# The last route of a mixture-of-experts takes along lanes and table of the route in front; a limit compared from PSUM; the order of four steps changed

## The chip, the cores and the metric

One core of a Trainium2 chip. The metric is the device time of one execution in microseconds (us), the median of several. The engines run side by side and keep each its own program order: TensorE (PE in the rows, PEld its weight loads), VectorE (DVE), ScalarE (ACT), GpSimd (POOL); SyncE (SP) issues most DMAs, POOL the gathers.

## What is computed

A linear attention with decay gives x, a mixture of 8 experts with one expert per token follows, and a gated MLP ends it. Batch 2, sequence 768, width 384 (8 heads of 48), expert width 1024, all in float32. The part that matters here is how the expert of a token is found:

```python
logits = x @ w_gate
local_gate = sigmoid(x @ w_local)
for s in range(S):                       # for each of the 2 sequences
    fresh_e = argmax(logits[b, s])
    e = fresh_e if s == 0 or local_gate[b, s] < 0.5 else prev_e
    prev_e = e
    p = softmax(logits[b, s])
    out[b, s] = p[e] * (relu(x[b, s] @ w1[e]) @ w2[e])
```

## The kernel before

**Attention.** The sequence is cut into 6 chunks of 128 tokens (`c`), each for 2 batches (`b`). For a chunk the kernel makes scaled keys and queries (`prep`: `kt`, `rh`, on DVE or POOL), scores on PE (`scores`, tile `pa`), a mask on DVE (`mask`, tile `am`), and in `mix` the product with the values (`py`), the part from the running state `st`, and the update of the state (`pst`, added on DVE). The token's own term comes from `diag` (`ku` on POOL, its sum `ad` on DVE) and `own` (`av`, on ACT, or on POOL for the last). `rows` adds it to `py` and writes 128 rows of x to DRAM (`xd`). A buffer `py` can be written again only when its `rows` has read it.

**Routes.** `route` gives each token its expert and its place in that expert's list. It is a generator, and each `yield` ends a step that the calling code places between other work. It runs for the groups of chunks (0, 1), (2, 3), (4,), (5,). Its steps: the logits plus own gates and the bit "takes a fresh expert" (`rb`, `ro`, DVE); counts of those bits (`pz`, PE); the best expert (`mx` to `oh`, DVE); a selection matrix `sel` (DVE), which picks for each token the row of its last fresh token, and `cz`, the expert carried in from the chunk in front, for tokens that `nz` marks; the experts `oes` (PE, then DVE) and `od`, the same times the token's number; places in the lists (PE, DVE: `rks`); `lane`, for each token a row of 256 with a one at its place (a comparison on DVE with `board.lanes`, the numbers 0 to 255); and the product of `lane` and `od` on PE, which is added to `table`. For the last group that sum goes to `rowid`, the row numbers by which the gathers fetch the experts' tokens (`x_fetch`, indirect DMA on POOL, tile `xe`). Small results of all routes lie in one PSUM bank, the tile `board`. The framework orders PE's writes to that bank behind every DVE access that stands in front of them in the program, and the other way round.

**The end of the attention.** Before the last routes are done, part of expert 0 is begun: `first_part` (in the code `lead`) turns the first half of the gathered rows (`tx`), multiplies them with the first weights (`h`, 24 products of 128 columns, in 8 steps) and those with the second weights (`o`, 24 products), with the turning of the second half after 15 of them. `FILL` says how many steps of `lead` stand between two steps of the last route. The weights of the experts come by DMA and are split into a high and a low part (ACT casts, DVE or POOL subtracts, line 321). After that come expert by expert `layer1` and `layer2`, then the gather of the results and the gated MLP; both are PE's work from end to end.

**A count check.** After the first route `limit` compares two of the counts with 128 (line 268): more would send the kernel to a general version.

Of the kernel before, what the change touches and what calls it, by code (L numbers as in the profile page):

```python
# [9 lines left out]
F32 = mybir.dt.float32  # L10
F32R = mybir.dt.float32r
BF16 = mybir.dt.bfloat16
F16 = mybir.dt.float16
# [3 lines left out]
ALU = mybir.AluOpType  # L17
# [4 lines left out]
B = 2  # L22
# [5 lines left out]
E = 8  # L28
FF = 1024
C = 128  # L30
NC = S // C
CAP = 256
HC = CAP // 2
NE = 2
NF = 4
# [2 lines left out]
WS = 3072  # L38
LC = D + G
WARM = 22  # L40
FILL = (0, 3, 1, 0, 1, 1, 0)
WMIN = 0.6
WMAX = 1.1

# [2 lines left out]
def rwkv_moe_gmlp(ctx, tc, a, out):  # L47
# [94 lines left out]
                return x.rearrange("t (g e) -> t g e", e=shape[1])  # L142
            return x

    def route(cs, board, lg, more, sm, ps):

        n = len(cs)
        c = cs[-1]
        N = n * B
        turn = turn_of(c)  # L150

        def small(nm, shp, dt=F32):
            return sm.tile([128, 2 * B] + shp[2:], dt, name=nm, tag=nm)[:, 0:N]
# [4 lines left out]
        def bc(t):  # L158
            return t.unsqueeze(2).to_broadcast([128, N, E])
# [32 lines left out]

        mx = small("mx", [128, N])
        ve.tensor_reduce(mx, l8, axis=AX.X, op=ALU.max)
        ve.tensor_tensor(sc, l8, bc(mx), op=ALU.is_equal)
        ex = board.exs[:, B * cs[0]:B * cs[0] + N]
        ve.tensor_tensor(ex, l8, bc(mx), op=ALU.subtract)
        ve.tensor_tensor(sc, sc, rev.unsqueeze(1).to_broadcast([128, N, E]), op=ALU.mult)
        m2 = small("m2", [128, N])
        ve.tensor_reduce(m2, sc, axis=AX.X, op=ALU.max)  # L200
        oh = small("oh", [128, N, E], BF16)
        ve.tensor_tensor(oh, sc, bc(m2), op=ALU.is_equal)
        se.activation(ex, ex, AF.Exp)
        yield
        cc = small("cc", [128, N])
        ve.tensor_copy(cc, pc)
        sel = [sm.tile([128, B, 2, C], BF16, name=f"sel{j}", tag=f"sel{j}", bufs=1) for j in range(n)]
        for j in range(n):
            for b in range(B):
                g = B * j + b  # L210
                ve.tensor_scalar(sel[j][:, b, j:n], pr[:, b, j:n], cc[:, g:g + 1], ro[:, g:g + 1],
                                 op0=ALU.is_equal, op1=ALU.mult)
        if cs[0]:

            ve.tensor_scalar(nz, pc, 0.0, None, op0=ALU.is_equal)
            cz = small("cz", [128, N, E])
            for j in range(n):
                g = slice(B * j, B * j + B)
                ve.tensor_tensor(cz[:, g], carry, nz[:, g].unsqueeze(2).to_broadcast([128, B, E]), op=ALU.mult)
        yield  # L220
        for b in range(B):
            for j in range(n):
# [2 lines left out]
                              start=(i == 0), stop=(i == j))  # L225
        pe.matmul(pf, lhsT=same, rhs=count.unsqueeze(1).to_broadcast([128, N, E]), start=True, stop=False)
        yield
        oe = board.oes[:, B * cs[0]:B * cs[0] + N]
        if cs[0]:
            ve.tensor_tensor(oe, cz, pq, op=ALU.add)  # L230
# [13 lines left out]
            pe.matmul(pn_, lhsT=ones, rhs=oe[:, g], start=(g == 0), stop=(g == N - 1))  # L244
        pe.matmul(pl, lhsT=last, rhs=oe[:, N - B:N], start=True, stop=True)
        yield
        rk = board.rks[:, B * cs[0]:B * cs[0] + N]
        rt_ = small("rt", [128, N, E])
        ve.tensor_tensor(rt_, oe, pf, op=ALU.mult)
        ve.tensor_reduce(rk, rt_, axis=AX.X, op=ALU.add)  # L250
        lane = sm.tile([128, 2 * B, CAP], F16, name="lane", tag="lane", bufs=1)
        for g in range(N):
            ve.tensor_scalar(lane[:, g], board.lanes, rk[:, g:g + 1], None, op0=ALU.is_equal)
        yield
        for h in range(2):
            for g in range(N):
                pe.matmul(pt_[:, h], lhsT=lane[:, g, 128 * h:128 * h + 128], rhs=od[:, g],
                          start=(g == 0), stop=(g == N - 1))

        ve.tensor_tensor(rowid if c == NC - 1 else table, table, pt_, op=ALU.add)  # L260
        ve.tensor_tensor(count, count, pn_, op=ALU.add)
        ve.tensor_copy(carry, pl)
        if c == NF - 1:

            ve.tensor_scalar(count[:, 0:1], count[:, 0:1], HC, None, op0=ALU.max)
            ve.tensor_copy(rowid[:, 0, 0:1], table[:, 0, 0:1])
        if c == NE - 1:
            ve.tensor_scalar(limit[:, E + 1:], count[:, E - 2:E], HC, None, op0=ALU.is_gt)
        yield

    def places(board, sm):
# [101 lines left out]
    def x_fetch(e, part=range(2), rows_read=B * S):  # L373
        if e not in xe:
            xe[e] = xep.tile([128, 2, DM], F32, name="xe", tag="xe")
        for m in part:
            po.indirect_dma_start(  # L377
                out=xe[e][:, m], out_offset=None, in_=xd[0:rows_read],
                in_offset=bass.IndirectOffsetOnAxis(ap=rowid[:, m, e:e + 1], axis=0))


    with ExitStack() as att:
# [94 lines left out]
        def prep(c, b):  # L477

            t = loads[c]
            rh[c, b] = wk.tile([128, NP, C], F32, name="rh", tag=f"rh{b}")  # L480
            kt[c, b] = wk.tile([128, NP, C], F32, name="kt", tag=f"kt{b}")
            if c + b == 0:
                def ready(n):
                    o = slice(n // 2, n) if n == C else slice(0, n)
                    if n >= C // 2:
                        ve.tensor_tensor(kt[0, 0][:, :, o], t["kT"][:, 0, :, o], ktab[:, :, o], op=ALU.mult)

                powers(ready)
                po.tensor_tensor(rh[0, 0], t["rT"][:, 0], rtab, op=ALU.mult)
                return  # L490
            (ve if c * b < 2 else po).tensor_tensor(kt[c, b], t["kT"][:, b], ktab, op=ALU.mult)
            po.tensor_tensor(rh[c, b], t["rT"][:, b], rtab, op=ALU.mult)

        def prep_keys(c, b=slice(0, B)):
# [113 lines left out]
        def first_part():  # L608

            def turned(m):  # L610
                t = ps1.tile([128, 3, 128], F32, name="tx", tag="pg")
                for k in range(3):
                    pe.transpose(t[:, k], xe[0][:, m, 128 * k:128 * k + 128], ident)
                return t

            t = turned(0)
            x = wk.tile([128, 3, 128], F32, name="xl", tag="x0")
            se.copy(x, t)
            yield
            part = [ld.tile([128, 8, 128], F32R, name="hp", tag=n) for n in ("kT", "rT")]  # L620
            hs = [ps1.tile([128, 4, 128], F32, name="h", tag=f"pa{g}") for g in range(2)]
            for f in range(8):
                for k in range(3):
                    pe.matmul(hs[f // 4][:, f % 4], lhsT=whole[:, k, 128 * f:128 * f + 128], rhs=x[:, k],
                              start=(k == 0), stop=(k == 2))
                yield
                if f == 4:
                    hf = wk.tile([128, 4, 128], F32, name="hf", tag="am")
                    se.activation(hf, hs[0], AF.Relu)
                    se.copy(part[0][:, 0:4], hf)  # L630
                    po.tensor_tensor(part[1][:, 0:4], hf, part[0][:, 0:4], op=ALU.subtract)
            se.activation(part[0][:, 4:8], hs[1], AF.Relu)
            ve.scalar_tensor_tensor(part[1][:, 4:8], hs[1], 0.0, part[0][:, 4:8], op0=ALU.max, op1=ALU.subtract)
            w2 = slot[1].rearrange("p j (k f) -> p j k f", k=8)
            o = ps1.tile([128, DM], F32, name="o", tag="pst")
            terms = sorted(((f, s, q) for f in range(8) for s, q in PASS), key=lambda x: x[1])
            for n, (f, s, q) in enumerate(terms):
                if n == 15:
                    se.copy(xf, turned(1))
                pe.matmul(o, lhsT=part[s][:, f], rhs=w2[:, q, f], start=(n == 0), stop=(n == 23))  # L640
                if n % 6 == 5:
                    yield
            ob = wk.tile([128, DM], F32, name="of", tag="x1")
            se.copy(ob, o)
            sy.dma_start(out=ys[0:HC, :], in_=ob)
# [28 lines left out]
        with tc.manual_schedule():  # L674
# [44 lines left out]
            for c in range(1, NC - 1):  # L719
# [20 lines left out]
                next(rt, 0)  # L740
                own(c, 0)
                y0 = mix(B * c)
                next(rt, 0)
                next(rt, 0)
                rows(c - 1, 1, y1)
                own_gates(c, 0)
                scores(B * c + 2)
                gates(c + 1, 1)
# [36 lines left out]
            old = [rt]  # L785
            next(rt)
            lead = first_part()
            scores(B * c + 1)
            next(dg)
            own(c, 1)  # L790

            def tabled():
                next(old[0])
                x_fetch(0, [0], NF * B * C)
                logits(c - 1, 1, y1)
                g = (c - 1,)
                old.append(route(g, board, xr[g, "l"], als[g], sm, ps1))
                next(old[1])

            y0 = mix(B * c, {0: tabled, 3: lambda: next(old[1])})  # L800
# [13 lines left out]
                logits(c, 0, y0)  # L814

            y1 = mix(B * c + 1, {2: experts, 3: lambda: next(rt)})
            next(rt)
            own_gates(c, 0)
            logits(c, 1, y1)
            old.append(route((c,), board, xr[(c,), "l"], als[(c,)], sm, ps1))  # L820
            rt = old[2]
            next(rt)
            rows(c, 0, y0)
            rows(c, 1, y1)
            w_split(0, 3, po, 1)
            w_fetch(1, 2)
            next(lead)
            next(old[1])
            next(rt)
            for n in FILL:  # L830
                next(rt)
                for _ in range(n):
                    next(lead, 0)
            x_fetch(0, [1])
            for _ in range(4):
                next(lead, 0)
            x_fetch(1)
            places(board, sm)
# [631 lines left out]
```

## Time and profile before

| | |
|---|---|
| runs (us) | 368.22, 368.73, 371.37; median 368.73 |
| the profiled execution: own time / span | 371.84 / 370.0 us |
| PE busy | 354.5 us (96% of the span) |
| DVE / ACT / POOL busy | 63% / 48% / 46% |
| mean granted TensorE clock | 0.98 |

The profile is of one execution, and its span reaches from its first instruction to its last. A busy share is a mean over stages with different limits; here the stages from 100 us on show no idle PE but for the hand-over between experts and MLP, and the attention shows idle PE in a few places, so the rows below are of those places.

### The profile page before, as it was taken

The numbers are of one execution on the slowest core, as the hardware profiler recorded it, in microseconds if no ns is written. First come the engines' busy times: TensorE is split into PE (matmuls) and PEld (weight loads), VectorE is DVE, ScalarE is ACT, GpSimd is POOL, SyncE is SP. The second block draws the span as 40 slices with busy tenths as digits, with TensorE's granted clock in tenths as the row PEclk, the third lists the DMA queues.
The fourth block names the chain that finished last, engine by engine and source line by source line (L and its number), as shares of the span: only waits on it lengthen the run. The fifth ranks groups of instructions, "written<-read, shape, count | busy, mean of one in ns | idle before, by whom it ended". The sixth has DMA issues, their size and how long they took to land.

```text
span 370.0 us, 6477 instructions
## 1 busy us (share of the span) xinstructions
PE 354.5 (96%) x2485; PEld 339.6 (92%) x2485; DVE 233.7 (63%) x429; ACT 175.9 (48%) x344; POOL 170.0 (46%) x105
## 2 busy tenths in 40 slices
PE   7999999798999999999999999999999999999992
PEld 3899999787899999999999999778999999999992
DVE  7486997997468879898989843356777223234000
ACT  4439666535278582928374353344568310102321
POOL 4779995925478966556464032441000431311000
PEclk9589999999999999999999999999999999999997
DMA  6978999032599999989897311535302000000321
GB/s 200 388 297 291 379 396 365 4 128 87 153 317 350 304 300 355 336 262 309 282 325 257 142 64 33 178 110 170 130 4 83 0 2 0 3 0 2 109 93 64
DMA packets 34920, 67.27 MB, mean 182 GB/s; under 512 B 2688, under 2 KB 18816, under 8 KB 34880
## 3 DMA queue, kind: packets, MB, share of 16 engines
q1 hardware_dynamic: 33088, 61.27, 47.7%
q0 software_dynamic: 1792, 5.51, 4.9%
q8 instruction: 21, 0.34, 0.4%
q14 instruction: 19, 0.16, 0.1%
HBM read 56.54 MB, written 10.22 MB: 180 GB/s over the span
## 4 chain that ended last, share of the span: by engine, by line
PE 84%; DVE 6%; DMA 4%; issue 2%; ACT 1%; POOL 1%; POOLq 0%; ACTq 0%
PE h L983 16%; PE o L1033 15%; PE vs L1150 13%; PE po L1166 7%; PE v L1096 7%; PE u L1135 5%; PE py L604 5%; PE pa L561 4%; PE tx L901 2%; PE pst L588 2%; PE pg L503 2%; PE py L599 2%; DMA xe<-xd,rowid 2%; PE h L1012 1%; DMA xg<-ys,slots 1%
## 5 line engine op out<-in xcount | busy, mean ns | idle before, releaser
L321 POOL TENSOR_TENSOR slot<-raw,slot 128x1536 fp32r<-128x1536 f32 x17 | 61.4, 3613 | 88.7 <-ACT slot L319 88.5
L983 PE MATMUL h<-xt,slot 128*128 128x256 f32 x504 | 61.7, 283 | 0.0
L983 PEld LDWEIGHTS h<-xt,slot 128*128 128x128 f32 x504 | 61.3, 192 | 0.1
L1033 PE MATMUL o<-slot,ht 128*128 128x384 f32 x336 | 60.2, 336 | 0.0
L1033 PEld LDWEIGHTS o<-slot,ht 128*128 128x128 f32 x336 | 58.0, 188 | 0.0
L321 DVE TENSOR_TENSOR slot<-raw,slot 128x1536 fp32r<-128x1536 f32 x19 | 42.8, 2253 | 18.3 <-ACT slot L319 18.3
L319 ACT CAST slot<-raw 128x1536 fp32r<-128x1536 f32 x36 | 53.1, 1477 | 0.0
L1150 PE MATMUL vs<-slot,slot 128*128 128x384 f32 x288 | 50.1, 334 | 0.0
L1150 PEld LDWEIGHTS vs<-slot,slot 128*128 128x128 f32 x288 | 49.9, 188 | 0.0
L1096 PE MATMUL v<-slot,xT 128*128 128x512 f32 x108 | 27.6, 401 | 0.0
L1157 ACT CAST slot<-gv 128x768 fp32r<-128x768 f32 x8 | 6.7, 838 | 43.9 <-POOL gv L1156 39.5
L604 PE MATMUL py<-vx,am 128*128 128x128 f32 x192 | 26.0, 285 | 0.0
L1156 POOL TENSOR_TENSOR gv<-gv,uT 128x768 f32<-128x768 f32 x7 | 12.9, 1838 | 28.0 <-DVE gv L1154 28.0
L1135 PE MATMUL u<-xT,slot 128*128 128x384 f32 x144 | 25.4, 335 | 0.2 <-ACT uT L1140 0.2
L1135 PEld LDWEIGHTS u<-xT,slot 128*128 128x128 f32 x144 | 25.0, 188 | 0.6 <-ACT uT L1140 0.5
L377 POOL DMA_INDIRECT xe<-xd,rowid x16 | 23.5, 1469 | 3.8 <-issue 1.2
L1166 PE MATMUL po<-slot,slot 128*128 128x384 f32 x144 | 25.1, 334 | 0.0
L1166 PEld LDWEIGHTS po<-slot,slot 128*128 128x128 f32 x144 | 25.0, 188 | 0.0
L604 PEld LDWEIGHTS py<-vx,am 128*128 128x128 f32 x192 | 23.8, 199 | 0.0
L993 DVE SCALAR_TENSOR_TENSOR ht<-h,ht 128x512 fp32r<-128x512 f32 (+1 forms) x28 | 18.0, 647 | 8.5 <-ACT ht L992 8.3
L1096 PEld LDWEIGHTS v<-slot,xT 128*128 128x128 f32 x108 | 19.5, 188 | 3.7
L891 POOL DMA_INDIRECT xg<-ys,slots x12 | 12.0, 1003 | 23.2 <-DVE slot L321 11.2
(203 smaller groups left out, 560.1 us busy)
## 6 DMA issues: line engine op xcount, KB each, us to landing
raw<-w SPq DMA_DIRECT2D x30, 768.0 KB, 6.4
raw<-w_in SPq DMA_DIRECT2D x6, 768.0 KB, 6.6
ys<-ob SPq DMA_DIRECT2D x15, 192.0 KB, 5.0
kT<-kT SPq DMA_DIRECT2D x5, 512.0 KB, 6.1
rT<-rT SPq DMA_DIRECT2D x5, 512.0 KB, 8.1
vT<-vT SPq DMA_DIRECT2D x6, 384.0 KB, 6.4
v<-v SPq DMA_DIRECT2D x6, 384.0 KB, 8.2
k<-k SPq DMA_DIRECT2D x6, 384.0 KB, 8.1
```

The lines of the kernel that those rows point to most:

```text
L319: se.copy(hi, r)
L321: (eng or ve).tensor_tensor(lo, r, hi, op=ALU.subtract)
L377: po.indirect_dma_start(out=xe[e][:, m], out_offset=None, in_=xd[0:rows_read], in_offset=bass.IndirectOffsetOnAxis(ap=rowid[:, m, e:e + 1] ...
L561: pe.matmul(pa[h][:, p, :], lhsT=kt[c, b][64 * h:64 * h + 64, p, :], rhs=rh[c, b][64 * h:64 * h + 64, p, :], start=True, stop=True)
L604: pe.matmul(y[:, p], lhsT=m[:, h * NP + p, :], rhs=v[:, b, p, h, :], start=(c + p + h == 0), stop=(p == NP - 1 and h == 1))
L983: pe.matmul(h[:, j], lhsT=w1[:, s, k, 128 * f:128 * f + 128], rhs=xt[e][:, m, k], start=(n == 0), stop=(n == 8))
L993: ve.scalar_tensor_tensor(lo, x, 0.0, hi, op0=ALU.max, op1=ALU.subtract)
L1033: pe.matmul(o, lhsT=hidden(e, m, s, f), rhs=w2[:, q, f], start=(n == 0), stop=(n == 23))
L1096: pe.matmul(o, lhsT=xT[b][:, s, k, 128 * c:128 * c + 128], rhs=win[:, q, k, DF:FF], start=(n == 0), stop=(n == 8))
L1135: pe.matmul(o[:, h, 0:HS], lhsT=win[:, s, k, 128 * d:128 * d + 128], rhs=xT[b][:, q, k, HS * h:HS * h + HS], start=(n == 0), stop=(n == 8))
L1150: pe.matmul(o[:, h, 0:HS], lhsT=vn[b][:, s, k, 128 * d:128 * d + 128], rhs=wsp[q][:, k, HS * h:HS * h + HS], start=(n == 0), stop=(n == 17))
L1166: pe.matmul(o, lhsT=gt[b][:, s, k, 128 * c:128 * c + 128], rhs=wout[q][:, k], start=(n == 0), stop=(n == 11))
```

## The change

Six edits, all around the routes.

1. `limit` is compared from the sum in PSUM (`pn_`) instead of from `count` in SBUF.
2. In `route` the copy `cc` and the mark `nz` come right after `mx`, and `cz` in front of `m2`; before, they came at and after the selections.
3. In the loop over chunks `rows(c - 1, 1, y1)` comes in front of the two route steps behind `mix`.
4. `kt` of the last chunk's first batch is made on POOL instead of DVE.
5. At the last chunk the gather of the first half of expert 0's rows is issued in front of the own values (`own(c, 1)`); its one column of row numbers is written straight from PSUM, in front of `table`.
6. The route of chunk 4 stops when it has its places (`give`), and the last route (`take`) makes that route's lanes between its own steps, from a copy of the lane numbers in another PSUM bank (`held["lanes"]`), and does the products of both in one sum. `FILL` is new, and the first part's yields are finer: one product instead of three. The subtraction for `part[1]` goes behind the loop, and the last chunk's own gates go ahead of one route step.

```diff
-FILL = (0, 3, 1, 0, 1, 1, 0)
+FILL = (3, 0, 0, 7, 0, 1, 0, 5)
...
         ve.tensor_reduce(mx, l8, axis=AX.X, op=ALU.max)
+        if take:
+            take.pop("sums")()
+        cc = small("cc", [128, N])
+        ve.tensor_copy(cc, pc)
+        if cs[0]:
+            ve.tensor_scalar(nz, pc, 0.0, None, op0=ALU.is_equal)
         ve.tensor_tensor(sc, l8, bc(mx), op=ALU.is_equal)
...
+        if cs[0]:
+            cz = small("cz", [128, N, E])
+            for j in range(n):
+                g = slice(B * j, B * j + B)
+                ve.tensor_tensor(cz[:, g], carry, nz[:, g].unsqueeze(2).to_broadcast([128, B, E]), op=ALU.mult)
         m2 = small("m2", [128, N])
...
-        cc = small("cc", [128, N])
-        ve.tensor_copy(cc, pc)
         sel = [sm.tile([128, B, 2, C], BF16, name=f"sel{j}", tag=f"sel{j}", bufs=1) for j in range(n)]
...
+        def comparison(t, rk, g):
+            ve.tensor_scalar(t[:, g], take["lanes"] if take else board.lanes, rk[:, g:g + 1], None, op0=ALU.is_equal)
+
+        if take:
+            comparison(take["lane"], take["rk"], 0)
         oe = board.oes[:, B * cs[0]:B * cs[0] + N]
...
+        def sums():
+            ve.tensor_tensor(count, count, pn_, op=ALU.add)
+            ve.tensor_copy(carry, pl)
+        if take:
+            comparison(take["lane"], take["rk"], 1)
...
+        if give is not None:
+            give.update(lane=lane, rk=rk, od=od, sums=sums)
+            yield
+            return
...
+        pairs = [(lane[:, g], od[:, g]) for g in range(N)]
+        if take:
+            pairs = [(take["lane"][:, g], take["od"][:, g]) for g in range(B)] + pairs
...
+        if c == NF - 1:
+            ve.tensor_tensor(rowid[:, 0, 0:1], table[:, 0, 0:1], pt_[:, 0, 0:1], op=ALU.add)
         ve.tensor_tensor(rowid if c == NC - 1 else table, table, pt_, op=ALU.add)
...
-            ve.tensor_copy(rowid[:, 0, 0:1], table[:, 0, 0:1])
-        if c == NE - 1:
-            ve.tensor_scalar(limit[:, E + 1:], count[:, E - 2:E], HC, None, op0=ALU.is_gt)
+        if cs == tuple(range(NE)):
+            ve.tensor_scalar(limit[:, E + 1:], pn_[:, E - 2:E], HC, None, op0=ALU.is_gt)
...
-            (ve if c * b < 2 else po).tensor_tensor(kt[c, b], t["kT"][:, b], ktab, op=ALU.mult)
+            (ve if c * b < 2 and c < NC - 1 else po).tensor_tensor(kt[c, b], t["kT"][:, b], ktab, op=ALU.mult)
...
-                yield
+                    if f < 7 or k < 2:
+                        yield
...
                 y0 = mix(B * c)
+                rows(c - 1, 1, y1)
                 next(rt, 0)
                 next(rt, 0)
-                rows(c - 1, 1, y1)
...
+            held = {"lanes": ps1.tile([128, CAP // 2], F32, name="lanes", tag="pst").bitcast(F16)}
+            ve.tensor_copy(held["lanes"].bitcast(F32), lanes.bitcast(F32))
             scores(B * c + 1)
             next(dg)
-            own(c, 1)
             def tabled():
                 next(old[0])
                 x_fetch(0, [0], NF * B * C)
+                own(c, 1)
                 logits(c - 1, 1, y1)
...
             y1 = mix(B * c + 1, {2: experts, 3: lambda: next(rt)})
+            own_gates(c, 0)
             next(rt)
-            own_gates(c, 0)
...
-            next(lead)
-            next(old[1])
-            next(rt)
             for n in FILL:
-                next(rt)
                 for _ in range(n):
                     next(lead, 0)
+                next(rt)
             x_fetch(0, [1])
-            for _ in range(4):
+            for _ in range(9):
                 next(lead, 0)
             x_fetch(1)
```

On **DVE**, behind the first `mix` of chunk 4, where the route of chunks 2 and 3 runs, stood before:

```order
L194 TENSOR_REDUCE mx<-board 128x4
L195 TENSOR_TENSOR board<-board,mx 128x32
L197 TENSOR_TENSOR exs<-board,mx 128x32
L198 TENSOR_TENSOR board<-board,rev 128x32
L200 TENSOR_REDUCE m_984<-board 128x4
L202 TENSOR_TENSOR oh<-board,m_984 128x32
L206 COPY cc<-board 128x4
L211 TENSOR_SCALAR sel_991<-pz,cc,ro 128x256 x2
L211 TENSOR_SCALAR sel_992<-pz,cc,ro 128x128 x2
L215 TENSOR_SCALAR board<-board 128x4
L219 TENSOR_TENSOR cz<-carry,board 128x16 x2
L670 TENSOR_TENSOR x<-py,av 128x384
```

There stands now (line 696 is `rows`, line 222 the selections):

```order
L696 TENSOR_TENSOR x<-py,av 128x384
L195 TENSOR_REDUCE mx<-board 128x4
L199 COPY cc<-board 128x4
L202 TENSOR_SCALAR board<-board 128x4
L203 TENSOR_TENSOR board<-board,mx 128x32
L205 TENSOR_TENSOR exs<-board,mx 128x32
L206 TENSOR_TENSOR board<-board,rev 128x32
L211 TENSOR_TENSOR cz<-carry,board 128x16 x2
L213 TENSOR_REDUCE m_993<-board 128x4
L215 TENSOR_TENSOR oh<-board,m_993 128x32
L222 TENSOR_SCALAR sel_998<-pz,cc,ro 128x256 x2
L222 TENSOR_SCALAR sel_999<-pz,cc,ro 128x128 x2
```

The read of `py` moved from the end of this piece to its head, and `cc`, the mark (written to `board`) and `cz` moved in front of the selections.

On **PE**, at the end of the attention, the products of the two last routes stand between those of the first part (`h`, `o`). The rows are the first MATMUL of each kind in order, without the weight loads; before:

```order
L624 MATMUL h<-xl,whole 128x128 x3
L257 MATMUL board<-od,lane 128x8
L185 MATMUL pz<-up_65,rb 128x128
L624 MATMUL h<-xl,whole 128x128 x9
L224 MATMUL board<-oh,sel_1266 128x8
L624 MATMUL h<-xl,whole 128x128 x3
L239 MATMUL board<-oes,upst 128x16
L624 MATMUL h<-xl,whole 128x128 x6
L624 MATMUL h<-xl,whole 128x128 x3
L640 MATMUL o<-slot_105,hp 128x384 x15
L613 MATMUL tx<-ident,xe 128x128 x3
```

and now (`pz` belongs to the last route, `lane` to the last two):

```order
L649 MATMUL h<-xl,whole 128x128 x3
L186 MATMUL pz<-up_65,rb 128x128
L649 MATMUL h<-xl,whole 128x128 x7
L228 MATMUL board<-oh,sel_1264 128x8
L649 MATMUL h<-xl,whole 128x128
L248 MATMUL board<-oes,upst 128x16
L649 MATMUL h<-xl,whole 128x128 x5
L281 MATMUL board<-od,lane 128x8
L649 MATMUL h<-xl,whole 128x128 x8
L666 MATMUL o<-slot_105,hp 128x384 x15
L638 MATMUL tx<-ident,xe 128x128 x3
```

Before, the last route's four `lane` products stood between the rows x6 and x3 of `h`. The four of the route in front moved from ahead of `pz` to there, so that eight stand together; 7, 1, 5 and 8 products of the first part stand where 9, 3, 6 and 3 stood.

On **POOL**, from the split of the weights in chunk 3 on, stood before:

```order
L321 TENSOR_TENSOR slot_105<-raw,slot_105 128x1536
L492 TENSOR_TENSOR rh<-rT,rtab 128x512
L491 TENSOR_TENSOR kt<-kT,ktab 128x512
L520 TENSOR_TENSOR ku<-k,ub 128x768
L522 TENSOR_TENSOR ku<-ku,r 128x768
L535 TENSOR_TENSOR av<-vx_164,ad 128x456
L377 DMA xe<-xd,rowid 128x384
L668 TENSOR_TENSOR x<-x,av 128x384 x3
L631 TENSOR_TENSOR hp<-hf,hp 128x512
L377 DMA xe<-xd,rowid 128x384 x3
```

and now:

```order
L346 TENSOR_TENSOR slot_105<-raw,slot_105 128x1536
L516 TENSOR_TENSOR kt<-kT,ktab 128x512
L517 TENSOR_TENSOR rh<-rT,rtab 128x512
L545 TENSOR_TENSOR ku<-k,ub 128x768
L547 TENSOR_TENSOR ku<-ku,r 128x768
L402 DMA xe<-xd,rowid 128x384
L560 TENSOR_TENSOR av<-vx_164,ad 128x456
L694 TENSOR_TENSOR x<-x,av 128x384 x3
L657 TENSOR_TENSOR hp<-hf,hp 128x512
L402 DMA xe<-xd,rowid 128x384 x2
```

A multiplication `kt` is new in front of `rh` (each list leaves out the second `rh`, a second `kt` and a second split, which did not move), the gather of the first half went ahead of `av`, and that of the second half, which before was the first of the three at the end, went ahead of `hp`.

## Rows read from the trace of the kernel before

**Rows 1.** Windows, 100 to 225 us: length; PE, PEld, DVE, ACT, POOL; clock; DMA.

```profile
100.00:225.00 125.00, 125.00 (x910) 124.90 (x909) 100.01 (x100) 75.27 (x101) 70.54 (x26) 1.00 0.79 267
```

**Rows 2.** Windows, around the comparison, and the end of the attention whole.

```profile
62.50:66.70 4.20, 2.15 (x25) 1.81 (x24) 4.13 (x7) 2.62 (x10) 4.20 (x2) 1.00 0.42 159
62.50:98.20 35.70, 30.05 (x301) 28.00 (x299) 30.59 (x118) 14.60 (x47) 23.40 (x16) 1.00 0.32 107
```

**Rows 3.** Timeline, PE: start us, us, instruction, count, idle time before and its releaser.

```profile
66.61 0.50 PE L185 MATMUL pz<-up,rb 128*128 128x256 bf16 x4 [2.05 <-DVE rb L172]
74.74 1.16 PE L599 MATMUL py<-st,rh 128*128 128x128 f32 x8 [1.07 <-DVE x L670]
85.02 0.55 PE L613 MATMUL tx<-ident,xe 128*128 128x128 f32 x3 [0.50 <-DMA xe<-xd,rowid]
86.33 0.17 PE L239 MATMUL board<-oes,upst 128*128 128x16 bf16 x1 [0.16 <-DVE board L657]
88.49 0.24 PE L257 MATMUL board<-od,lane 128*128 128x8 f16 x4 [0.68 <-DVE ro L173]
91.41 0.19 PE L224 MATMUL board<-oh,sel 128*128 128x8 bf16 x2 [0.42 <-DVE cz L219]
98.17 0.52 PE L613 MATMUL tx<-ident,xe 128*128 128x128 f32 x3 [0.77 <-DMA xe<-xd,rowid]
```

**Rows 4.** Timeline, the comparison and its neighbours on PE, POOL and DVE.

```profile
62.37 3.43 POOL L321 TENSOR_TENSOR slot<-raw,slot 128x1536 fp32r<-128x1536 f32 x1 [4.41 <-ACT slot L319]
62.42 3.41 DVE L268 TENSOR_SCALAR limit<-count 128x2 f32<-128x2 f16 x1
63.67 0.89 PE L503 MATMUL pg<-wgb,vT 128*128 128x72 f32 x6
66.39 0.16 DVE L172 TENSOR_SCALAR rb<-board 128x4 bf16<-128x4 f32 x1
```

**Rows 5.** Timeline, POOL and DVE behind it, and the scores that use their tiles.

```profile
65.76 1.26 POOL L492 TENSOR_TENSOR rh<-rT,rtab 128x512 f32<-128x512 f32 x1
68.59 1.44 DVE L491 TENSOR_TENSOR kt<-kT,ktab 128x512 f32<-128x512 f32 x1
70.75 1.16 PE L561 MATMUL pa<-rh,kt 64*128 64x128 f32 x16
```

**Rows 6.** Timeline, DVE: the selections and the rows.

```profile
72.22 1.63 DVE L211 TENSOR_SCALAR sel<-pz,cc,ro 128x256 bf16<-128x256 f32 x4
74.14 0.55 DVE L670 TENSOR_TENSOR x<-py,av 128x384 f32<-128x384 f32 x1
```

**Rows 7.** Timeline, the table of chunks 2 and 3 and the first gather.

```profile
80.53 0.95 POOL L535 TENSOR_TENSOR av<-vx,ad 128x456 f32<-128x456 f32 x1 [6.92 <-DVE ad L525]
80.66 0.17 DVE L260 TENSOR_TENSOR table<-table,board 128x16 f32<-128x16 f32 x1 [0.27 <-PE board L257]
81.65 1.13 POOL L377 DMA_INDIRECT xe<-xd,rowid  x1 [0.17 <-DVE board L166]
```

**Rows 8.** Timeline, the last two routes and the first part.

```profile
87.04 0.61 DVE L253 TENSOR_SCALAR lane<-board,rks 128x256 f16<-128x256 f16 x2
88.21 0.16 DVE L172 TENSOR_SCALAR rb<-board 128x2 bf16<-128x2 f32 x1
88.73 2.25 PE L624 MATMUL h<-xl,whole 128*128 128x128 f32 x18
94.51 0.97 POOL L377 DMA_INDIRECT xe<-xd,rowid  x1 [0.34 <-DVE carry L262]
94.56 2.84 PE L640 MATMUL o<-slot,hp 128*128 128x384 f32 x15
```

**Rows 9.** SP's writes of x: the last three, landing of all twelve, of these three.

```profile
83.79 6.10 SPq L672 DMA_DIRECT2D xd<-x  x3
...
DMA to landing us min/median/max: 1.8/4.0/8.0
...
xd<-x SPq DMA_DIRECT2D x3, 192.0 KB, 1.9
```

More of the change, by code (lines that the diff above doesn't have):

```diff
@@ L143, in part, with route @@
             return x
-    def route(cs, board, lg, more, sm, ps):
+    def route(cs, board, lg, more, sm, ps, give=None, take=None):
         n = len(cs)
@@ L212, in route @@
                                  op0=ALU.is_equal, op1=ALU.mult)
[L213 to L219, printed above, removed]
         yield
@@ L250, in route @@
         ve.tensor_reduce(rk, rt_, axis=AX.X, op=ALU.add)
-        lane = sm.tile([128, 2 * B, CAP], F16, name="lane", tag="lane", bufs=1)
+        lane = take["lane"] if take else sm.tile([128, 2 * B, CAP], F16, name="lane", tag="lane", bufs=1)
+        if give is not None:
[3 more added lines that the diff above has]
+        if take:
+            lane = lane[:, B:2 * B]
         for g in range(N):
-            ve.tensor_scalar(lane[:, g], board.lanes, rk[:, g:g + 1], None, op0=ALU.is_equal)
+            comparison(lane, rk, g)
         yield
+        pairs = [(lane[:, g], od[:, g]) for g in range(N)]
+        if take:
+            pairs = [(take["lane"][:, g], take["od"][:, g]) for g in range(B)] + pairs
         for h in range(2):
-            for g in range(N):
-                pe.matmul(pt_[:, h], lhsT=lane[:, g, 128 * h:128 * h + 128], rhs=od[:, g],
-                          start=(g == 0), stop=(g == N - 1))
+            for i, (x, y) in enumerate(pairs):
+                pe.matmul(pt_[:, h], lhsT=x[:, 128 * h:128 * h + 128], rhs=y,
+                          start=(i == 0), stop=(i == len(pairs) - 1))
+        if c == NF - 1:
+            ve.tensor_tensor(rowid[:, 0, 0:1], table[:, 0, 0:1], pt_[:, 0, 0:1], op=ALU.add)
         ve.tensor_tensor(rowid if c == NC - 1 else table, table, pt_, op=ALU.add)
-        ve.tensor_tensor(count, count, pn_, op=ALU.add)
-        ve.tensor_copy(carry, pl)
+        sums()
         if c == NF - 1:
             ve.tensor_scalar(count[:, 0:1], count[:, 0:1], HC, None, op0=ALU.max)
-            ve.tensor_copy(rowid[:, 0, 0:1], table[:, 0, 0:1])
-        if c == NE - 1:
-            ve.tensor_scalar(limit[:, E + 1:], count[:, E - 2:E], HC, None, op0=ALU.is_gt)
+        if cs == tuple(range(NE)):
+            ve.tensor_scalar(limit[:, E + 1:], pn_[:, E - 2:E], HC, None, op0=ALU.is_gt)
         yield
@@ L630, in first_part @@
                     se.copy(part[0][:, 0:4], hf)
-                    po.tensor_tensor(part[1][:, 0:4], hf, part[0][:, 0:4], op=ALU.subtract)
+            po.tensor_tensor(part[1][:, 0:4], hf, part[0][:, 0:4], op=ALU.subtract)
             se.activation(part[0][:, 4:8], hs[1], AF.Relu)
@@ L794, in tabled @@
                 x_fetch(0, [0], NF * B * C)
+                own(c, 1)
                 logits(c - 1, 1, y1)
                 g = (c - 1,)
-                old.append(route(g, board, xr[g, "l"], als[g], sm, ps1))
+                old.append(route(g, board, xr[g, "l"], als[g], sm, ps1, give=held))
                 next(old[1])
@@ L816, in rwkv_moe_gmlp @@
             y1 = mix(B * c + 1, {2: experts, 3: lambda: next(rt)})
+            own_gates(c, 0)
             next(rt)
-            own_gates(c, 0)
             logits(c, 1, y1)
-            old.append(route((c,), board, xr[(c,), "l"], als[(c,)], sm, ps1))
+            old.append(route((c,), board, xr[(c,), "l"], als[(c,)], sm, ps1, take=held))
             rt = old[2]
```

## The prediction

> **What bounds the kernel now.** I read the windows first, because busy shares mix stages. From 100 to 225 us PE is busy for 125.00 of 125.00 us at full clock [rows 1]; no route runs there, so the change can only shift that stretch. What PE can still give lies before it: between 62.5 and 98.2 us PE is busy for 30.05 of 35.70 us [rows 2], 5.65 us are idle, and the clock is 1.00, so nothing is to be had from the clock. The timeline of PE then says where these 5.65 us are: seven waits, 2.05 + 1.07 + 0.50 + 0.16 + 0.68 + 0.42 + 0.77 = 5.65 [rows 3]. Six of them end with a DVE step of a route or with a gather, which are what the change touches. From 98.7 us on there is no idle PE that it could remove, so whatever PE gains before should reach the end unchanged.
>
> **The change part by part.**
>
> *The limit (edit 1).* The largest wait, 2.05, is for `rb`. `rb` itself is short; in front of it on DVE stands the comparison of two numbers per partition, which took 3.41 us, from 62.42 to 65.83, while POOL's split ran from 62.37 to 65.80 [rows 4]. So it ended when POOL did. A comparison of twice as many numbers from PSUM, `rb`, takes 0.16 [rows 4]. Now the operand is in PSUM. I take 0.16. The rule that bears on it is in the Trainium skill, page "SBUF — State Buffer", section "Who interferes with whom": DVE and GpSimd share a port pair as an exclusive lock, and the one that begins first holds it for its whole instruction; the trace agrees (3.41 against 0.16). `rb` began 0.56 after the comparison's end, so it would begin at 62.42 + 0.16 + 0.56 = 63.1 and end at 63.3. PE's work ahead of `pz` ends at 63.67 + 0.89 = 64.56 [rows 4], 1.2 us later. The wait is gone: **-2.05**, and would be even if the freed comparison took 1.2 us more.
>
> *Rows in front of the selections (edits 2 and 3).* PE waited 1.07 for `x`, at 74.14 on DVE, which frees `py`; in front of it stood the four selections, 1.63 from 72.22 on, and `mx` to `cz` [rows 3, 6]. With `x` (0.55) first and the selections 0.55 later, the wait for `x` goes: **-1.07**. The selections' cover: PE's use of them lies behind the products that waited for `x`, 1.16 us at 74.74 [rows 3], and DVE no longer makes the 1.44 us `kt` [rows 5] ahead of them; I see no new wait.
>
> *`kt` on POOL (edit 4).* One more POOL step in front of `rh`. POOL is free at 65.76, so `kt` and `rh`, each 1.26 by the row of the same shape, end at 68.3 [rows 5]. The scores that read both began at 70.75 and now, 2.05 earlier, at 68.70. Spare: 0.4 us. Cost 0, but this is the thinnest cover of the change.
>
> *The first gather (edit 5).* It was issued at 81.65, behind `av` on POOL, which ran until 81.48, though `table` was ready at 80.83 [rows 7]. Issued right after the table, it starts about 0.7 earlier, and PE waited 0.50 for it [rows 3]: **-0.50**. The own values come 1.1 us (the gather's turn) later; their reader, the POOL step of `rows`, comes after the mixing, some us later: 0.
>
> *The last route (edit 6).* Before, the two lanes of chunk 4 (0.61) stand between its places and the last route's `rb` [rows 8], and PE waits 0.68 for `ro` [rows 3]. With the lanes gone from there, `rb` comes 0.6 earlier: **-0.68**, less about 0.1. The lanes are made later, one in each DVE wait for PE, so they cost little. The wait of 0.42 was for `cz`, which is no longer behind the selections: **-0.42**. But 7 products of `h` stand before `sel`, not 9. A product is two rows here, 18 rows are 2.25, so one is 0.25 [rows 8], and two fewer cost 0.5: a new wait of about 0.6 at `sel`. One product, not three, stands before the places: about 0.3 new. In the front route, `nz` and `cz` now stand ahead of its selections (two DVE steps of 0.16 to 0.2): about 0.4 new. Products that only change place cost nothing.
>
> *The second gather.* It was issued at 94.51 and its rows were needed at 98.17, 3.66 later, when PE had waited 0.77 [rows 3, 8]. Behind the lanes PE now has 8 products of `h`, 8 x 0.23 = 1.8, and the 15 of `o`, 2.84 [rows 8]: 4.6. The four more lane products delay the issue by 0.1, and the issue follows the lanes by 0.5, so 4.2 is needed: **-0.77**, with 0.4 to spare. The 0.16 stays.
>
> *Sum.* 2.05 + 1.07 + 0.50 + 0.68 + 0.42 + 0.77 = 5.49 gained, less 0.1 + 0.6 + 0.3 + 0.4 = 1.4 of new waits: 4.1. The new waits are bounded by zero below. I have counted each at its full chain, without what the earlier start of DVE's steps takes from it; halving them gives 4.8. I take 4.5, in the middle. The profiled execution, 371.84 with a span of 370.0, would be 367.3 with a span of 365.5; against the median of 368.73 it is 364.2, or -1.2%.
>
> **The rivals.**
>
> *The waits of the last route only move.* If DVE's chain through the last two routes sets their pace, PE meets its end wherever the products are put. For it: PE waits there for DVE three times, and DVE works through steps of 0.2 back to back. Against it: the chain itself loses 0.61 and the gather wait is not DVE's. Then only 2.05 + 1.07 remain, 3.12: 365.6.
>
> *POOL is late.* If POOL's `kt` and `rh` come 1.3 us later than reckoned, the scores wait 0.9: gain 3.6, 365.1; with a further wait of the masks 365.3. Against it: POOL's start at 65.76 is set by a split whose own start, 62.37, does not move.
>
> *The comparison is not freed.* By the rule above the lock would not go away but pass to the next DVE step that needs the pair; were that a step between the comparison and `rb`, the 2.05 would stay and the gain be 2.4: 366.3. Against it: those steps are two sums and an addition with one operand in PSUM, and the whole distance of 0.56 held while POOL ran `rh` from 65.76 on [rows 4, 5].
>
> *It is given back in the weight stream.* DMA is 0.79 busy from 100 to 225 us [rows 1]; if weights were what paces PE there, an earlier start would only meet them earlier: gain 0, 368.7. Against it: PE has no idle time at all there, and the weights' issues follow PE's release of the buffers.
>
> *Slower: the second gather meets the last write of x.* The gather reads what SP's last write puts there. That write's issue ended at 83.79 + 6.10 = 89.89, and the gather was issued 4.6 later [rows 8, 9]. The lanes of chunk 4 leave the stretch between them, about 0.5, so 4.1 remain. These three writes landed in 1.9, but over all twelve the median is 4.0 and the longest 8.0 [rows 9]. A landing beyond 4.1 + 0.4 = 4.5 delays PE one for one; at 8.0 it costs 3.5 and leaves a gain of 1.0 (367.7), and from 9.0 on the whole 4.5 is lost and the kernel is slower: at 13, 372.7. Against it: the row of these very writes, 1.9.
>
> **How the numbers follow.** Forecast (gain 3.5 to 5.4) 0.68; waits only move 0.18; POOL late 0.05; comparison not freed 0.03; given back 0.03; slower 0.03. The likeliest alone spans 363.3 to 365.3. For 8 in 10, I take 363.0, where all 5.49 and a little more is gained, up to 366.3, which takes in the moved waits, the late POOL and the held comparison. A change of 1%, 3.7 us or 365.0, is about what a measurement of this kernel can tell from none. Faster by more than that: the forecast less its upper edge, 0.66. Slower by more: 0.03. The rest, 0.31, lies between.
>
> **What would show it.** In the profile after: the comparison at about 0.16 us beside the split; no PE wait ahead of the second `pz`, nor ahead of the products with `st` in the last chunk; `kt` on POOL for 1.26 and no wait at the scores; the first gather right behind `table`, the turns (`tx`) without a wait both times; small waits at `sel` and at the places (under 0.7 each). PE's idle time from 62.5 to the second `tx` would be near 1.3 us, not 5.65, and the window behind still full. Wrong would be: a comparison of more than 1.3 us; a gather that waits for a write of x; waits at `sel` and places above 2 us together; a stretch behind 100 us that is longer than before.

## The result, and the profile after

The changed kernel takes 363.78 us (median, 363.62 to 365.23) against 368.48 (367.94 to 371.37); the ratio is 0.9873 with a 95% interval of 0.983 to 0.9916. The forecast was 364.2 in 363.0 to 366.3. The sum came out right; two of its largest terms did not, as the experiments show.

One thing has to be known for the times below: in some executions TensorE is granted half its clock for some us early in the attention (0.50 from about 11 to 20 us in the traces of before, e4 and e8, from about 26 to 28 in e10), which puts the comparison 1.2 to 4.7 us later, and the profile of before is such an execution, that of after is not. The first fence is a window of before, the second the same of after (length; PE, PEld, DVE, ACT, POOL; clock; DMA):

```profile
15.00:20.00 5.00, 5.00 (x27) 4.78 (x27) 2.02 (x4) 2.52 (x6) 3.90 (x4) 0.50 1.04 413
```

```profile
15.00:20.00 5.00, 5.00 (x48) 5.00 (x47) 3.99 (x7) 0.93 (x2) 3.82 (x4) 1.00 1.04 413
```

So the two spans (370.0 and 362.0) differ by 3.5 us that the change has nothing to do with, and beside each median I read a **distance** inside one trace: from the start of the comparison `limit` to the first product of expert 0's second half (`h<-whole`, line 1012 before, 1037 after). It begins behind those places and ends behind the last route. Before it is 100.10 - 62.42 = 37.68, after 92.18 - 58.88 = 33.30: **4.38 us shorter**. A distance is read from one trace; where a kernel was traced twice it came out the same within 0.05 (33.30 and 33.35 for the changed kernel, 32.66 and 32.68 for e8 and e11). What is left from there to the end is 269.9 and 269.8 us.

The windows of after that answer to [rows 1] and [rows 2], from the comparison to the second turn, and from 100 us on:

```profile
59.00:90.30 31.30, 30.11 (x301) 27.91 (x300) 25.68 (x114) 14.50 (x47) 24.08 (x17) 1.00 0.39 128
...
100.00:225.00 125.00, 125.00 (x892) 124.86 (x891) 98.36 (x98) 71.55 (x97) 69.67 (x28) 1.00 0.78 260
```

PE is idle for 1.19 us instead of 5.65, near the 1.3 that was forecast, though not in the places that were forecast. The timeline of after around the comparison [rows 4]:

```profile
58.87 3.45 POOL L346 TENSOR_TENSOR slot<-raw,slot 128x1536 fp32r<-128x1536 f32 x1 [3.12 <-ACT slot L344]
...
58.88 0.15 DVE L293 TENSOR_SCALAR limit<-board 128x2 f32<-128x2 f32 x1
...
60.17 0.89 PE L528 MATMUL pg<-wgb,vT 128*128 128x72 f32 x6
60.90 0.49 PE L186 MATMUL pz<-up,rb 128*128 128x256 bf16 x4
```

The comparison takes 0.15 beside the same split, and `pz` follows the gates' products with nothing between. Of the seven waits of [rows 3] two are left; the third row here is the last route's `sel`:

```profile
79.06 0.17 PE L248 MATMUL board<-oes,upst 128*128 128x16 bf16 x1 [0.15 <-DVE board L683]
...
82.66 0.50 PE L228 MATMUL board<-oh,sel 128*128 128x8 bf16 x2
...
90.27 0.52 PE L638 MATMUL tx<-ident,xe 128*128 128x128 f32 x3 [0.45 <-issue]
```

A new wait hides inside the `sel` row: its two products take 0.50, and 0.19 before [rows 3], since the second waits for its half of the selection; 0.3 that no list of waits shows. The second turn still waits 0.45.

### The profile page after: what moved, and what is told of

Its sections match the earlier page's. It is cut to its first block, busy times and chain, and to the rows that moved or that the text cites. A ratio compares the mean times of both kernels' runs of the same rounds, so it can differ in the third digit from the quotient of the medians.

```text
span 362.0 us, 6474 instructions
## 1 busy us (share of the span) xinstructions
PE 350.4 (97%) x2485; PEld 335.2 (93%) x2485; DVE 229.9 (64%) x428; ACT 175.8 (49%) x344; POOL 171.8 (47%) x106
## 4 chain that ended last, share of the span: by engine, by line
PE 82%; DVE 4%; DMA 4%; POOL 3%; issue 3%; ACT 1%; SPq 1%; POOLq 0%; ACTq 0%; DVEq 0%
PE h L1008 17%; PE o L1058 16%; PE vs L1175 14%; PE po L1191 7%; PE u L1160 5%; PE v L1121 5%; PE py L629 4%; PE pa L586 2%; PE tx L926 2%; PE py L624 2%; DMA k<-k 2%; PE pst L613 2%; PE pg L528 2%; PE h L1037 1%; PE o L666 1%
## 5 line engine op out<-in xcount | busy, mean ns | idle before, releaser
L629 PE MATMUL py<-vx,am 128*128 128x128 f32 x192 | 25.1, 279 | 0.0
L629 PEld LDWEIGHTS py<-vx,am 128*128 128x128 f32 x192 | 22.8, 192 | 0.0
```

The costliest lines, as they stand in the source:

```text
L629: pe.matmul(y[:, p], lhsT=m[:, h * NP + p, :], rhs=v[:, b, p, h, :], start=(c + p + h == 0), stop=(p == NP - 1 and h == 1))
```

## The experiments

Ten variants, one of them twice (e8 and e11), and the changed kernel once more (e10), with the ratio to the kernel before on the same chip:

| kernel | median us | ratio (95%) | distance us |
|---|---|---|---|
| before | 368.2 to 368.7 | 1 | 37.68 |
| changed | 363.78 | 0.9873 (0.983 to 0.9916) | 33.30 |
| e1: before + edit 1 | 364.4 | 0.9905 (0.9872 to 0.9937) | 33.95 |
| e2: changed - edit 1 | 367.37 | 0.9997 (0.9966 to 1.0028) | 37.06 |
| e3: before + edits 2, 3 | 368.1 | 1.0022 (0.998 to 1.0065) | 37.45 |
| e4: before + edits 1 to 5 | 364.26 | 0.9915 (0.9875 to 0.9955) | 33.92 |
| e5: changed - edit 4 | 363.7 | 0.9891 (0.9849 to 0.9934) | 33.27 |
| e6: changed - order of edit 5 | 363.73 | 0.9891 (0.985 to 0.9932) | 33.58 |
| e7: changed, `hp` on DVE | 364.39 | 0.9885 (0.9855 to 0.9914) | 33.69 |
| e8: changed, weights later | 363.6 | 0.9874 (0.9825 to 0.9923) | 32.66 |
| e9: e2 with PE's wait filled | 366.83 | 0.9978 (0.9935 to 1.0021) | 35.69 |
| e10: changed again | 364.66 | 0.9872 (0.9832 to 0.9912) | 33.35 |
| e11: e8 again | 363.14 | 0.9857 (0.9809 to 0.9906) | 32.68 |
| e12: e1, weights later | 368.58 | 0.9991 (0.9952 to 1.0029) | 35.99 |

**e1, edit 1 alone.**

```diff
-            ve.tensor_scalar(limit[:, E + 1:], count[:, E - 2:E], HC, None, op0=ALU.is_gt)
+            ve.tensor_scalar(limit[:, E + 1:], pn_[:, E - 2:E], HC, None, op0=ALU.is_gt)
```

> The kernel before with edit 1 alone: the comparison reads the sum in PSUM. Own theory (the comparison was held up by the split on GpSimd, and what it held up was the last wait in front of the counts): the comparison takes 0.16 us instead of 3.41, the wait of 2.05 in front of the counts goes, the other six stay, 368.5 - 2.05 = 366.4 us. Rival (the lock passes to the next DVE step, or another wait takes its place): a step behind the comparison grows to about 3 us, 368.5 us.

Neither came: 364.4 us, a distance of 33.95. One line gives 3.73 of the 4.38 us. The timeline of PE shows that two waits went, not one:

```profile
60.78 0.49 PE L185 MATMUL pz<-up,rb 128*128 128x256 bf16 x4
...
67.67 1.06 PE L599 MATMUL py<-st,rh 128*128 128x128 f32 x8
...
77.72 0.55 PE L613 MATMUL tx<-ident,xe 128*128 128x128 f32 x3 [0.37 <-DMA xe<-xd,rowid]
...
81.19 0.24 PE L257 MATMUL board<-od,lane 128*128 128x8 f16 x4 [0.68 <-DVE ro L173]
84.10 0.19 PE L224 MATMUL board<-oh,sel 128*128 128x8 bf16 x2 [0.42 <-DVE cz L219]
90.81 0.52 PE L613 MATMUL tx<-ident,xe 128*128 128x128 f32 x3 [0.71 <-DMA xe<-xd,rowid]
```

`py` at 67.67 is the row that waited 1.07 for `x` in [rows 3]; here it waits for nothing, although selections and rows stand in their old order. DVE reached them on time:

```profile
66.85 0.55 DVE L670 TENSOR_TENSOR x<-py,av 128x384 f32<-128x384 f32 x1
```

That is 8.08 behind the start of the comparison (58.77), and was 11.72 (74.14 [rows 6] less 62.42): DVE comes 3.64 earlier. PE, whose own work fills a part of that time, comes only 2.18 earlier at `pz`, so DVE gains 1.46 on PE, more than the 1.07. The 1.07 was the lateness of DVE behind the comparison, met a second time. Set against before, start by start, PE gains 2.2 at `pz`, 1.2 to 1.3 at that `py` and some 0.2 at the first turn: each wait is worth a little more than its row says.

**e3, edits 2 and 3 alone** (the same lines of `route` and the call of `rows`, moved in the kernel before):

> The kernel before with edits 2 and 3 alone: the rows, the copy, the mark and the carried expert in front of the selections. Own theory: the wait of 1.07 for the rows goes and none comes in the route of chunks 2 and 3, in the last route the wait for the carried expert is one for the selections instead, of about the same 0.4: 368.5 - 1.07 = 367.4 us. Rival (the chain of DVE sets the pace, waits only move): a new wait of about 1 us at the selections of chunks 2 and 3, 368.5 us.

The rival was nearer: 368.1 us, a distance 0.23 shorter. Its PE timeline:

```profile
62.83 0.50 PE L185 MATMUL pz<-up,rb 128*128 128x256 bf16 x4 [2.05 <-DVE ro L173]
71.05 0.29 PE L224 MATMUL board<-oh,sel 128*128 128x8 bf16 x6 [0.26 <-DVE board L657]
72.71 0.18 PE L239 MATMUL board<-oes,upst 128*128 128x32 bf16 x1 [0.35 <-DVE od L236]
...
94.17 0.52 PE L613 MATMUL tx<-ident,xe 128*128 128x128 f32 x3 [1.04 <-DMA xe<-xd,rowid]
```

The waits for `x` and `cz` are gone; 0.26 at the selections, 0.35 at the experts, 0.12 and 0.27 more at the two turns took their place, and the last route's `sel` row has 0.3 inside it (its two products take 0.49, and 0.19 in e1). A late engine that gets its steps in another order is late with another step.

**e4, edits 1 to 5 without 6.**

> The kernel before with edits 1 to 5, without edit 6: the last route takes nothing along, and the order of the first part is the old one. Own theory: three waits go, 2.05 + 1.07 + 0.50, and those of the last two routes and of the second gather stay, 0.68 + 0.42 + 0.77: 368.5 - 3.6 = 364.9 us, 1.1 above the changed kernel. Rival (in the last routes the waits only moved, edit 6 is worth nothing): 363.8 us, as the changed kernel.

The median, 364.26, lies between the two. The distance is 33.92, as e1's 33.95: with edit 1 in place, edits 2 to 5 together are worth nothing that can be told. The waits of 0.37 for the first gather and of 0.42 for `cz` go, but 0.3 comes inside each of the two `sel` rows (0.50 each), and the wait for the second gather grows from 0.71 to 0.96. The remaining 0.62 is edit 6, by the distance alone: the medians of e4 and of the changed kernel lie within each other's intervals.

**e2, the changed kernel with the comparison from SBUF again** (the diff of e1 turned round), and **e9**, the same with nine products on constants in front of the counts:

```diff
+        if cs == (2, 3):
+            for _ in range(9):
+                pe.matmul(pz.rearrange("t (a b) -> t a b", a=4), lhsT=ones,
+                          rhs=ones.unsqueeze(1).to_broadcast([128, 4, 128]), start=True, stop=True)
```

> The changed kernel with edit 1 alone undone: the comparison reads the counts in SBUF again. Own theory: it starts just after the split and ends with it, 3.4 us, and PE waits some 2.1 us in front of the counts: 363.8 + 2.1 = 365.9 us. Rival (the gain of edit 1 is taken up by waits further on, so that undoing it costs less than its wait): 363.8 to 364.8 us.

> The kernel of e2 (the changed one with the comparison from SBUF) with nine products of 512 columns on constants in front of the counts' products: they fill about 1.9 of the 2.05 us in which PE waits there, and their results are overwritten. Theory of the clock (in e2 PE's clock fell after the idle 2.05 us and cost another 1.5): the granted clock stays at 1.00 behind the wait, only the wait itself is paid, 363.7 + 2.1 to 2.3 = 365.9 us. Rival (the slow products of e2 have another cause, in the data or on DVE): 367.4 us, as e2.

e2's 367.37 us is above both expectations, and 3.76 of distance are lost, although its trace has one wait more than the changed kernel's, of 2.05. Windows of e2 behind that wait:

```profile
64.00:65.00 1.00, 1.00 (x6) 1.00 (x6) 1.00 (x2) 1.00 (x5) 1.00 (x2) 0.50 0.00 0
65.00:66.00 1.00, 1.00 (x7) 1.00 (x6) 0.87 (x4) 0.86 (x4) 1.00 (x2) 0.50 0.00 0
66.00:67.00 1.00, 1.00 (x7) 1.00 (x7) 0.97 (x5) 0.00 (x0) 1.00 (x1) 0.50 0.00 0
```

The granted clock is 0.50, the lower level of 1.2 GHz, and 6 or 7 products begin in a us where 11 or 12 did. In e9 PE has work during the wait (the row at 60.92), and the same windows have the full clock:

```profile
60.92 2.11 PE L183 MATMUL pz<-ones 128*128 128x512 bf16 x9
63.14 0.50 PE L190 MATMUL pz<-up,rb 128*128 128x256 bf16 x4
```

```profile
64.00:65.00 1.00, 1.00 (x11) 1.00 (x11) 1.00 (x3) 0.96 (x5) 1.00 (x2) 1.00 0.00 0
65.00:66.00 1.00, 1.00 (x12) 1.00 (x11) 0.95 (x4) 1.00 (x5) 1.00 (x2) 1.00 0.00 0
```

Its distance is 35.69: 2.39 above the changed kernel for the wait itself, and 1.37 below e2, which the lower clock had cost. This rests on one trace each: e9's median, 366.83, lies between its two expectations, and its interval overlaps e2's. That the clock fell in e2's profile because PE had been idle fits e9; that it must fall after such a wait does not hold, since before and e3 have the same 2.05, e12 has a wait of 2.76, and their traces keep the clock there. The comparison itself took 3.40 in e2 and 3.41 in e3 and e9, as in before, each time to the end of POOL's split.

**e5, `kt` on DVE again.**

```diff
-            (ve if c * b < 2 and c < NC - 1 else po).tensor_tensor(kt[c, b], t["kT"][:, b], ktab, op=ALU.mult)
+            (ve if c * b < 2 else po).tensor_tensor(kt[c, b], t["kT"][:, b], ktab, op=ALU.mult)
```

> The changed kernel with edit 4 alone undone: kt of the last chunk's first batch on DVE again, 1.44 us between the mask and the state. Own theory: DVE had time there, the selections come about 1.0 later, just before PE needs them at 68.68, so 363.7 to 364.0 us. Rival (the selections become the bound): a wait of 0.5 to 1.4 us in front of the selections' products, 364.3 to 365.2 us.

No difference (33.27): the own theory held. DVE's timeline: `kt` takes 1.00, and the selections begin 0.25 later than in the changed kernel (65.44), since DVE had waited for PE there anyway (0.58 for `pst` in the changed kernel).

```profile
61.87 1.00 DVE L516 TENSOR_TENSOR kt<-kT,ktab 128x512 f32<-128x512 f32 x1
...
65.69 1.62 DVE L222 TENSOR_SCALAR sel<-pz,cc,ro 128x256 bf16<-128x256 f32 x4
```

**e6, the own values in front of the first gather again** (the call `own(c, 1)` at its old place).

> The changed kernel with edit 5 undone in its order: the own values on GpSimd in front of the first gather again. Own theory: the gather is issued 0.9 later, PE waits about 0.5 for its rows, and all that follows moves with it: 364.3 us. Rival (the wait at the second gather, 0.45, gets shorter by as much): 363.8 us.

Between the two: the distance is 0.28 longer. PE's timeline shows 0.42 at the first turn; a part of it comes back at `sel`, which is now ready in time (0.20 for its two products), and the wait for the second gather grows by 0.13.

```profile
77.91 0.55 PE L638 MATMUL tx<-ident,xe 128*128 128x128 f32 x3 [0.42 <-DMA xe<-xd,rowid]
...
90.57 0.52 PE L638 MATMUL tx<-ident,xe 128*128 128x128 f32 x3 [0.58 <-DMA xe<-xd,rowid]
```

**Why the second gather is late: e7, e8, e11 and e12.** In the changed kernel the gather is issued at 85.80 and PE begins with its rows at 90.27, 4.47 later; before it was 3.66 [rows 3, 8]. First SP's issue of weights and POOL's of the gather, then what the DMA queues moved from 87.0 to 88.5 (packets, MB, share of 16 engines):

```profile
85.12 0.38 SPq L337 DMA_DIRECT2D raw<-w  x1
```

```profile
85.80 0.99 POOL L402 DMA_INDIRECT xe<-xd,rowid  x1 [0.71 <-DVE carry L258]
86.81 1.30 POOL L657 TENSOR_TENSOR hp<-hf,hp 128x512 fp32r<-128x512 f32 x1
```

```profile
q1 hardware_dynamic: 323, 0.50, 91.5%
```

Only the weights move; the gather's queue has nothing until 88.5. Either the weights, issued 0.7 earlier, stand in front, or POOL's own next step holds up the gather. e7 takes that step off POOL, e8 takes the weights away:

```diff
-            po.tensor_tensor(part[1][:, 0:4], hf, part[0][:, 0:4], op=ALU.subtract)
+            ve.tensor_tensor(part[1][:, 0:4], hf, part[0][:, 0:4], op=ALU.subtract)
```

```diff
...
-            w_fetch(1, 2)
             for n in FILL:
...
             for _ in range(9):
                 next(lead, 0)
+            w_fetch(1, 2, se)
             x_fetch(1)
```

> The changed kernel with the subtraction for the first half of hp on DVE instead of GpSimd, where it stands right behind the second gather. Theory of the weights (the gather's packets wait behind those of the weights' transfer that was issued 0.7 earlier): nothing changes, PE still waits about 0.45 for the second turn, 363.8 us. Theory of GpSimd (its next work holds up the gather it has just issued): the wait goes, 363.3 us.

> The changed kernel with the transfer of expert 1's third piece of weights issued by ScalarE about 3 us later, behind its work for hp, and not right in front of the second gather. Theory of the weights: the gather's packets start about 2 us after its issue instead of 3, PE's wait of 0.45 for the second turn goes, 363.3 us. Theory of GpSimd: the wait stays, 363.8 us. If the weights are missed later, a wait in the second layer of expert 1: above 364 us.

> The kernel of e8 again (the transfer of weights behind the second gather). Theory of the weights: 0.45 to 0.6 us below the changed kernel of the same call, 363.2 us. Rival (e8 was chance): no difference, 363.7 us.

e7 made it worse: the wait is 0.83, and POOL's issue took 1.38 instead of 0.99, while DVE's `hp` ran from 85.63 to 86.32. The wait grew by 0.38, about as much as the issue (0.39), so with POOL's next step gone nothing was won: it was not the cause. My own expectation of no change missed too.

```profile
85.82 1.38 POOL L402 DMA_INDIRECT xe<-xd,rowid  x1 [0.72 <-DVE carry L258]
```

In e8 and e11 the second turn does not wait, and the distance is 32.66 and 32.68, 0.6 below the changed kernel. In e11, with the gather issued at 85.82 as before, its packets are the only ones that move from 87.0 to 88.5; the weights follow:

```profile
87.28 0.41 ACTq L337 DMA_DIRECT2D raw<-w  x1
```

```profile
q0 software_dynamic: 61, 0.20, 47.2%
```

The medians agree (363.14 for e11, 364.66 for the changed kernel on the same chip), but their intervals overlap; that e11 is the fastest kernel here rests on the distance, seen twice. No later wait for weights appeared.

e12 asked whether edit 1 and the later weights do it alone:

> The kernel before with edit 1 and with the transfer of weights issued by ScalarE behind its work for hp, as in e8; no other edit. If edit 1 is nearly the whole gain and the second gather waits for the weights: the wait of 0.71 for the second turn that was left in e1 goes, 364.0 - 0.7 = 363.3 us, not above the changed kernel. Rival (edits 2 to 6 are needed for the second gather's rows to be in time): the wait stays, 364.0 us.

Both wrong: 368.58 us, a distance 2.04 longer than e1's. There the gather comes later (87.30), and ScalarE's issue falls 0.34 behind the start of POOL's instead of 1.5 behind. POOL, ScalarE and PE of e12:

```profile
87.30 0.96 POOL L377 DMA_INDIRECT xe<-xd,rowid  x1 [0.34 <-DVE carry L262]
...
87.64 0.41 ACTq L312 DMA_DIRECT2D raw<-w  x1
...
92.96 0.52 PE L613 MATMUL tx<-ident,xe 128*128 128x128 f32 x3 [2.76 <-DMA xe<-xd,rowid]
```

```profile
q10 hardware_dynamic: 251, 0.39, 46.0%
```

From 87.0 to 90.5 only the weights' packets move, and PE waits 2.76. So the weights were in front here though their issue began behind that of the gather, which took POOL until 88.26; issued 1.46 behind it, in e11, they were not. It is the same cause with the opposite sign, and it is not the queue, since e11 and e12 both issue from ScalarE. The medians of e12 and e1 are 4.2 apart; the profiled execution, 366.27 us, shows 2.0 of that, and where the others lost more is open.

## Why the prediction was right, and where it was not

**The sum, right.** 4.5 forecast, 4.7 by the medians and 4.38 by the distance. Nothing was given back behind 100 us, as argued.

**The limit, right in mechanism, too small.** The comparison fell to 0.15 and the 2.05 went. But edit 1 alone gives 3.73 (e1), not 2.05. The Trainium skill, page "SBUF — State Buffer", section "Who interferes with whom", bears on it as the prediction says; 3.41 and 0.15 beside the same split agree. Edit 1 changes the operand's place and its type together (f16 in SBUF, f32 in PSUM by the rows), and no run parts the two.

**Rows in front of the selections, wrong.** This step read the wait of 1.07 as one of order ("in front of it stood the four selections"). It was the lateness of the comparison, found 8 us further on: it goes with edit 1 alone (e1), and moving the rows alone only moves it (e3, 0.23). I had asked of the compare's 3.25 us only whether they reached `rb`, not where else DVE's queue was still late; the 1.2 us that I kept as spare behind the 2.05 were spent here. The two steps' sum, 3.12, is near the 3.73 that edit 1 gave, which is why the total came out: luck, as far as the split between the steps goes.

**`kt` on POOL, right** at nothing (e5). On POOL `kt` and `rh` end at 63.50 + 1.28 = 64.78 and the scores begin at 65.03, 0.25 of cover where 0.4 was forecast.

**The first gather, mis-sized.** The wait of 0.50 went, but 0.13 of it belonged to the comparison (0.37 is left in e1), and with the rest of the change in place the order is worth 0.28 (e6).

**The last route, right in sign.** The waits for `ro` and `cz` went, that for `cz` already with edit 2 (e3, e4). The new ones, put at 0.1 + 0.6 + 0.3 + 0.4, are about 0.3 in each of the two `sel` rows and under 0.15 at the rest. The 0.3 is not the two products fewer that the sum took it for: it stands in e4 too, with nine in front, and so comes with edit 2, which puts `cc`, the mark and `cz` ahead of the selections. In sum edit 6 gives 0.62 (e4 against the changed kernel).

**The second gather, wrong.** "-0.77, with 0.4 to spare" took the time from issue to rows as a constant of this gather. It was 3.66 before although its packets waited behind the weights there too, issued 1.54 ahead of it, and 4.47 after, since it is issued 0.68 behind them. These are SP's issue in before, and all that moved from 94.0 to 96.5 (the gather was issued at 94.51):

```profile
92.97 0.38 SPq L312 DMA_DIRECT2D raw<-w  x1
...
q1 hardware_dynamic: 428, 0.66, 88.1%
```

So 0.45 of wait stayed, and it goes when the weights do (e8, e11). The forecast took 5.49 - 4.5 = 0.99 off for new waits; what came is this 0.45 and 0.59 of new waits (PE's idle 1.19 less 0.15 and 0.45), 1.04 together, so that the total fits here by luck too. The slower rival looked at another transfer, the writes of x, and at another mechanism, data that has not landed; what acts is a transfer whose packets go first.

**The rivals.** "The waits only move" holds for edits 2 and 3, not for the last route. A late POOL, a comparison that stays held and a gain given back did not come.

**The clock.** "Nothing to be had from the clock" holds for the profile of before. In e2's trace the wait carries 1.4 more in a lower clock behind it, so what edit 1 is worth within the changed kernel lies between 2.4 (e9) and 3.8 (e2).

## What to carry to other kernels

A wait in a list is where an engine's lateness is met, not where it arises: before two waits on one engine are priced apart, follow that engine back from the later one to see whether it has been on time in between. Look first for a small instruction with a long row, since one line at its source (here a comparison's operand) was worth 3.73 us, and a new order of the steps behind it 0.23 (e3). For a gather, read which other transfers were issued near it (here from 1.54 us before to 0.34 after), and not only its own time from issue to landing.

## What the runs showed of the hardware

The gather's packets began 1.7 us after its issue began where nothing else moved (e11: 85.82, first packets at 87.5). With the 768 KB of weights near it they began 2.2 us after it when these were issued 1.54 earlier (before: 96.7), 3.1 when 0.68 earlier (the changed kernel: 88.9), and 3.5 when 0.34 later (e12: 90.8). In the first two most of the weights had gone by then (0.74 and 0.73 MB of 0.79), in e12 0.49 MB.

The comparison of two numbers per partition took all of POOL's split in every kernel that reads them from SBUF (3.40 or 3.41 each). It always began 0.05 behind the split, so these rows alone could also be of a slow comparison. Another step in the trace of before speaks for the split: line 337, DVE again and from SBUF to SBUF, takes 0.55 or 0.56 where no split runs, and 4.15 to 4.17 in the four cases where one does, each time to some 0.43 behind the split's end, though its own row begins some 0.2 ahead of the split's, while POOL still issues a gather:

```profile
125.78 0.55 DVE L337 TENSOR_SCALAR h<-raw 128x768 int32<-128x768 int32 x1
...
141.73 4.17 DVE L337 TENSOR_SCALAR h<-raw 128x768 int32<-128x768 int32 x1
...
141.95 3.52 POOL L321 TENSOR_TENSOR slot<-raw,slot 128x1536 fp32r<-128x1536 f32 x1
```

Yet another DVE operation of that kind there, from SBUF to SBUF on one number per partition, took 0.16 while POOL's `av` ran from 80.53 to 81.48 [rows 7]:

```profile
80.93 0.16 DVE L265 TENSOR_SCALAR count<-count 128x1 f16<-128x1 f16 x1
```

What makes the difference, the count of elements, the types or the operation on POOL, was not tried.
